# Batch 0's two v loads move ahead of the identity in GpSimd's queue

## The chip, the cores and the metric

The kernel runs on one core of a Trainium2 chip. A core has engines that run side by side, each with its own stream of instructions in order: TensorE (PE, with its weight loads shown as PEld), VectorE (DVE), ScalarE (ACT), GpSimd (POOL) and SyncE (SP). Transfers between main memory and the core's own memory are issued by SP, ACT or GpSimd, each into a queue of its own, and are carried out by the core's 16 DMA engines. The metric is the device time of one execution in microseconds; the time before is the median of three runs, 201.05 us.

## What is computed

Linear attention over 8 batches and 8 heads (sequence 576, head size 64), and behind it a channel-mixing layer (512 to 1024 to 512). Cut to what matters:

```python
q_s = softmax(q, axis=-1)              # over the head's 64 columns
k_s = softmax(k, axis=2)               # over the 576 positions
kv  = einsum('bhsd,bhse->bhde', k_s, v)
x   = einsum('bhsd,bhde->bhse', q_s, kv)   # -> [8, 576, 512]

x_prev = x moved down by one position
xk = mu_k * x + (1 - mu_k) * x_prev
xr = mu_r * x + (1 - mu_r) * x_prev
k  = maximum(xk @ w_k, 0)
out = sigmoid(xr @ w_r) * ((k * k) @ w_v)
```

## The kernel before

The work is cut by batch `b` (0 to 7) and by group `g` (0 or 1, each of four heads in two halves 0 and 1). Every piece of work is an operation with a name: `load01q0` is the load of batch 0, group 1, q, half 0; `load00v` and `load01v` are batch 0's two v loads (a whole group each, into the tiles `vb_a` and `vb_b`, converted to bf16 on the way). `expq`, `rsum`, `rrec` and `scale` make the softmax of q; `expk` the exponentials of k; `KV`, `Z` and `T` are matmuls and transposes on TensorE; `X` makes the mixed attention output; `k`, `r` and `v` with a unit number are the matmuls of the channel-mixing layer.

The order of all operations is written out by hand in one string, `ORDER` (line 42). Each token is an operation, in the form `ENGINE!name:place^held`. The program walks through it and emits each operation on its engine, so the string sets the order within each engine's stream. An engine works its stream in order; between engines, semaphores hold an operation back until what it reads is there. Tokens of different engines that stand beside each other in the string do not wait for one another because of that.

At the start these engines have the following to do, each in this order:

- **SP** issues `load01q0`, `load00q0`, `load01q1`, `load00k0`, `load01k1`.
- **ACT** issues the two loads of the mu rows (`rows`), then `load00q1`, `load00k1`, `load01k0`. Then come a table load and a one-element exponential (`warm`, L228), which reads a tile that VectorE sets to zero, and the exponentials of q and k (L326) as their data arrive.
- **GpSimd** builds the 128 by 128 identity (`ident`, L253: a memset and an affine select, in `masks.py`), then issues `load00v` and `load01v` (L217), `load10q0` (raw_e), and further on four loads of w_k and the loads of batch 1 and of the other weights.
- **VectorE** runs `consts` (L235: four memsets and the cast of `pick`, which reads the identity), `zero` (L230: `warm` and `still`), and `late` (L243), and then the sums and scalings of q.
- **TensorE** runs fillers (L292: matmuls on the tile `still`, whose results nobody reads), the product `wide` (L262, which reads `pick` and the mu rows) after the fifth of them, one more filler that is held until batch 0's first reciprocal is done, and more fillers held by exponentials and sums, up to `KV000`.

The raw input tiles are raw_a and raw_b for batch 0's q, raw_c for group 0's k, and raw_d for group 1's k. Batch 0's transposes of q on TensorE read the identity too (L361). The v loads are read by `KV000`, `KV001` (vb_a) and `KV010`, `KV011` (vb_b), at L391.

Of the kernel before, what the change touches and what calls it, by code (L numbers as in the profile page):

```python
# [8 lines left out]
ACT = mybir.ActivationFunctionType  # L9
# [30 lines left out]
FIRST = ((0, 0), (0, 1), (1, 0), (1, 1))  # L40

ORDER = """
ACT!rows ident load01q0:0 load00q0:1 ACT!load00q1 load01q1 load00v consts ACT!load00k1:2 load00k0
ACT!load01k0:3 load01v zero late fill:3 warm load10q0:4 fill.2:2 fill.3:3 wk11 fill.4:2 fill.5:3
wk00 expq000:0 wide:0 load10q1 load01k1 rsum000:0 wk01 rrec000 expq011:1 scale000:0 wk10 expq010
fill.6^rrec000:3 rsum011:1 fill.7^expq011:2 expq001 fill.8^expq010:3 rsum010 fill.9^rsum011:2
fill.31:2 rsum001 fill.10^expq001:3 expk000:0 fill.11^rsum010:2 rrec010 widecopy scale010:1
# [771 lines left out]
```

## Time and profile before

| what | value |
|---|---|
| median of 3 runs | 201.05 us (200.26, 201.05, 202.83) |
| span of the profiled execution | 199.1 us |
| TensorE busy | 187.2 us |
| DMA, 0 to 20 us | 254 GB/s |
| DMA, 40 to 60 us | 400 GB/s |
| DMA, 100 to 120 us | 70 GB/s |

The span runs from the first instruction to the last one of the profiled execution. The profile gives no other time for that execution; the runs were timed without it, and their median is 1.95 us above its span. The median carries what lies around the span as well.

Where each of batch 0's loads stands in the profile (issue: start of the issuing instruction; landing: as the profile gives it from issue):

| tile | queue | issue, us | to landing, us |
|---|---|---|---|
| raw_a (2 loads) | SP | 0.74 and 1.65 | 6.6 (median) |
| raw_b | SP | 1.19 | 3.3 |
| raw_b | ACT | 1.59 | 6.4 |
| raw_c | ACT | 1.99 | 8.6 |
| raw_c | SP | 2.17 | 8.6 |
| raw_d | ACT | 2.49 | not given |
| raw_d | SP | 3.72 | not given |
| vb_a | GpSimd | 1.44 | 9.4 |
| vb_b | GpSimd | 2.29 | 11.2 |

In lines of the profile, `out<-in` are the tiles written and read; a bracket at the end of a timeline line holds the idle time of the engine just before the instruction, and what ended it. Engine idle time costs something only where the end of the kernel hangs on it.

### The profile page before, as it was taken

Reading aid. Unit: us, or ns where it says so; the run is one execution under the profiler, and the core shown is the slowest. Engines: PE = TensorE matmul, PEld = TensorE weight load, DVE = VectorE, ACT = ScalarE, POOL = GpSimd, SP = SyncE. Lnnn points to the kernel's source line nnn. Section 1 sums busy time; section 2 is a strip of 40 time slices with the busy share of each in tenths; the row PEclk is TensorE's granted clock in tenths of the full one; section 3 lists DMA queues with packets and bytes.
Section 4 is the critical chain, followed back from the end, with each engine's and each line's share of the span. In section 5 each row is a group of like instructions: output and inputs, shape, how many; then the busy total and the mean of one; then the engine's idle time right before and its main releaser. Section 6 shows DMA issues by size and latency. Waiting matters only on the chain.

```text
span 199.1 us, 5164 instructions
## 1 busy us (share of the span) xinstructions
PE 187.2 (94%) x2059; PEld 92.3 (46%) x2085; DVE 150.8 (76%) x348; ACT 145.7 (73%) x224; POOL 43.6 (22%) x70
## 2 busy tenths in 40 slices
PE   6598999989999999999999999999999999999992
PEld 2045445434444444445565545544444544444751
DVE  1588486889989999999999995999825459732531
ACT  3377798799999999999999488777624762552340
POOL 8435438954424312622000000000000000000000
PEclk9999999999999999999999999999999999999999
DMA  6999999999999998799942130422044013402513
GB/s 199 256 276 281 279 336 230 367 397 393 415 393 395 400 407 328 243 412 405 376 116 54 45 90 0 102 63 54 3 105 107 0 23 85 105 2 53 121 40 105
DMA packets 16544, 40.13 MB, mean 202 GB/s; under 512 B 2300, under 2 KB 5640, under 8 KB 16520
## 3 DMA queue, kind: packets, MB, share of 16 engines
q0 software_dynamic: 9440, 27.99, 42.3%
q1 hardware_dynamic: 6400, 10.65, 19.5%
q10 hardware_dynamic: 680, 1.15, 1.6%
q8 instruction: 16, 0.26, 0.6%
q14 instruction: 8, 0.07, 0.1%
HBM read 33.56 MB, written 9.44 MB: 216 GB/s over the span
## 4 chain that ended last, share of the span: by engine, by line
PE 50%; issue 1%; ACT 0%; DVE 0%
PE mm_c L653 7%; PE mm_d L653 6%; PE mm_d L601 5%; PE mm_c L601 4%; PE mm_a L653 4%; PE mm_b L601 4%; PE mm_a L601 4%; PE mm_b L633 3%; PE mm_b L653 3%; PE mm_a L633 3%; PE mm_d L633 2%; PE mm_c L633 1%; PE att_b L517 1%; PE att_a L517 1%; PE att_a L391 1%
## 5 line engine op out<-in xcount | busy, mean ns | idle before, releaser
L653 PEld LDWEIGHTS <-k_a 128*128 128x128 bf16 x144 | 13.8, 98 | 16.9 <-DVE k_a L592 0.6
L633 PEld LDWEIGHTS <-xr 128*128 128x128 bf16 x144 | 13.9, 98 | 16.4 <-issue 0.2
L653 PEld LDWEIGHTS <-k_b 128*128 128x128 bf16 x152 | 14.3, 98 | 15.0 <-issue 0.6
L633 PE MATMUL mm_b<-wr,xr 128*128 128x512 bf16 x45 | 12.2, 379 | 0.2
L601 PEld LDWEIGHTS <-wk_bb 128*128 128x128 bf16 x80 | 7.8, 98 | 7.7
L601 PEld LDWEIGHTS <-wk_ba 128*128 128x128 bf16 x80 | 7.7, 98 | 7.8 <-issue 0.3
L601 PEld LDWEIGHTS <-wk_ab 128*128 128x128 bf16 x80 | 7.6, 98 | 8.0 <-DVE xk L489 0.5
L601 PEld LDWEIGHTS <-wk_aa 128*128 128x128 bf16 x80 | 7.4, 98 | 8.3 <-issue 1.0
L633 PE MATMUL mm_a<-wr,xr 128*128 128x512 bf16 x39 | 10.2, 379 | 0.1
L588 ACT ACTIVATE rel_a<-mm_b 128x512 bf16<-128x512 f32 (+1 forms) x10 | 5.8, 576 | 5.9 <-PE mm_b L601 5.9
L588 ACT ACTIVATE rel_c<-mm_c 128x512 bf16<-128x512 f32 (+1 forms) x11 | 6.6, 598 | 1.2 <-PE mm_c L601 1.2
L633 PE MATMUL mm_c<-wr,xr 128*128 128x512 bf16 x28 | 7.2, 379 | 0.0
L592 DVE TENSOR_TENSOR k_b<-rel_a 128x512 bf16<-128x512 bf16 (+1 forms) x13 | 5.2, 401 | 2.4 <-ACT rel_a L588 2.0
L633 PE MATMUL mm_d<-wr,xr 128*128 128x512 bf16 x27 | 7.0, 379 | 0.0
L592 DVE TENSOR_TENSOR k_a<-rel_c 128x512 bf16<-128x512 bf16 (+1 forms) x14 | 5.7, 404 | 1.6 <-ACT rel_c L588 1.5
L592 DVE TENSOR_TENSOR k_b<-rel_c 128x512 bf16<-128x512 bf16 (+1 forms) x14 | 5.4, 387 | 1.8 <-ACT rel_c L588 1.4
L292 PE MATMUL mm_d<-still 128*128 128x512 bf16 x8 | 4.7, 592 | 2.1 <-DVE still L233 1.9
L592 DVE TENSOR_TENSOR k_a<-rel_b 128x512 bf16<-128x512 bf16 (+1 forms) x12 | 4.9, 404 | 2.4 <-ACT rel_b L588 2.4
L588 ACT ACTIVATE rel_c<-mm_b 128x512 bf16<-128x512 f32 (+1 forms) x6 | 3.5, 578 | 4.3 <-PE mm_b L601 4.3
L292 PE MATMUL mm_c<-still 128*128 128x512 bf16 x8 | 4.5, 611 | 2.2 <-ACT eq_b L326 2.2
L601 PE MATMUL mm_c<-xk,wk_ab 128*128 128x512 bf16 (+1 forms) x22 | 6.1, 361 | 0.3 <-DVE xk L489 0.2
L592 DVE TENSOR_TENSOR k_a<-rel_a 128x512 bf16<-128x512 bf16 (+1 forms) x14 | 5.4, 388 | 1.2 <-ACT rel_a L588 1.1
(358 smaller groups left out, 555.2 us busy)
## 6 DMA issues: line engine op xcount, KB each, us to landing
out_dram<-th_a SPq DMA_DIRECT2D x13, 128.0 KB, 4.6
out_dram<-th_b SPq DMA_DIRECT2D x12, 128.0 KB, 4.0
out_dram<-th_c SPq DMA_DIRECT2D x10, 128.0 KB, 2.8
out_dram<-th_d SPq DMA_DIRECT2D x10, 128.0 KB, 2.4
out_dram<-th_e SPq DMA_DIRECT2D x10, 128.0 KB, 3.9
raw_k<-in_v_dram POOLq DMA_DIRECT2D x2, 576.0 KB, 6.9
raw_a<-in_q_dram POOLq DMA_DIRECT2D x2, 576.0 KB, 10.0
raw_b<-in_q_dram POOLq DMA_DIRECT2D x2, 576.0 KB, 9.9
```

Source lines behind the costliest of these rows:

```text
L292: return kn.nc.tensor.matmul(kn.bank(slot), lhsT=kn.still[:, 0:128], rhs=kn.still[:], start=True, stop=True)
L391: kn.nc.tensor.matmul(kn.half(slot, r)[two[u], KVO:KVO + n], lhsT=kn.eks[ek.index][two[r], j, u, :], rhs=by, start=(j == 0), stop=(j == J ...
L517: kn.nc.tensor.matmul(kn.half(slot, u)[two[r], to:to + n], lhsT=kn.ws[w.index][two[u], r, :], rhs=kn.qts[qt.index][two[u], r, 64 + at:64 + ...
L588: kn.nc.scalar.activation(out=kn.rels[rel.index][:, 0:n], in_=kn.bank(kf)[:, 0:n], func=ACT.Relu, scale=HALF_ROOT)
L592: kn.nc.vector.tensor_tensor(out=kn.k2s[k2.index][:, fc, 0:n], in0=kn.rels[rel.index][:, 0:n], in1=kn.rels[rel.index][:, 0:n], op=ALU.mult)
L601: kn.nc.tensor.matmul(kn.bank(kf)[:, 0:n], lhsT=kn.wk[fc // 4][ct % 2][:, ct // 2, (fc % 4) * 128: (fc % 4) * 128 + 128], rhs=kn.xs[0][:, ...
L633: kn.nc.tensor.matmul(kn.bank(rps), lhsT=kn.xs[1][:, ct, c:c + 128], rhs=kn.wr[:, ct, :], start=(ct == 0), stop=(ct == CT - 1))
L653: kn.nc.tensor.matmul(kn.bank(vps)[:, 0:width], lhsT=kn.k2s[k2.index][:, ft, 128 * m:128 * m + 128], rhs=wv_of(ft)[:, part], start=(ft == ...
```

## The change

In `ORDER`, the token `ident` moves from the second place to behind `load01v`, and `load01v` moves up to stand right behind `load00v`. GpSimd's stream then begins with the two v loads, and the identity follows. All loads of GpSimd keep their order among each other, as do those of SP and ACT; the streams of VectorE and TensorE stay as they are.

```diff
 ORDER = """
-ACT!rows ident load01q0:0 load00q0:1 ACT!load00q1 load01q1 load00v consts ACT!load00k1:2 load00k0
-ACT!load01k0:3 load01v zero late fill:3 warm load10q0:4 fill.2:2 fill.3:3 wk11 fill.4:2 fill.5:3
+ACT!rows load01q0:0 load00q0:1 ACT!load00q1 load01q1 load00v load01v ident consts ACT!load00k1:2
+load00k0 ACT!load01k0:3 zero late fill:3 warm load10q0:4 fill.2:2 fill.3:3 wk11 fill.4:2 fill.5:3
```

## The prediction

> **What bounds the kernel now.** I read the page's engine table and the chain of waits first, then the busy time by stage, the timeline of the first 20 us, who waited for whom, and the DMA queues window by window.
>
> ```profile
> PE 187.2 (94%) x2059; PEld 92.3 (46%) x2085; DVE 150.8 (76%) x348; ACT 145.7 (73%) x224; POOL 43.6 (22%) x70
> ...
> PE 50%; issue 1%; ACT 0%; DVE 0%
> ```
>
> TensorE is busy 94% of the span and the chain that ended last consists of matmuls. By stage:
>
> ```profile
> 0.00:20.00 20.00, 14.78 (x216) 6.71 (x220) 12.09 (x47) 11.40 (x18) 10.46 (x21) 1.00 1.00 254
> 20.00:40.00 20.00, 19.90 (x231) 9.58 (x232) 14.61 (x36) 16.96 (x29) 13.20 (x22) 1.00 1.08 303
> ```
>
> The columns are the stage, its length, the busy time of PE, PEld, DVE, ACT and POOL with counts, the clock, the DMA share and GB/s. From 20 us on PE has no room (19.90 of 20). Only before that does it wait, and the DMA share there is 1.00: the start waits for data, and the end of the kernel moves with the moment at which the dense part begins. So I ask which load that moment hangs on.
>
> ```profile
> 8.31 1.26 ACT L326 ACTIVATE eq_b<-raw_a 128x576 bf16<-128x576 f32 x2 [3.12 <-DMA raw_a<-in_q_dram]
> ...
> 13.19 1.26 ACT L326 ACTIVATE ek_b<-raw_d 128x576 bf16<-128x576 f32 x2 [0.62 <-DMA raw_d<-in_k_dram]
> 14.35 1.10 ACT L369 COPY qt_a<-att_b 128x1152 bf16<-128x1152 bf16 x1
> ```
>
> Each line has start, length, instruction, and in brackets the idle time and what ended it. The last k loads (raw_d) release ScalarE at 13.19; then come its copy at 14.35, the first K·V product of group 1 on PE at 14.69, and everything behind. The two v loads are not in this chain: vb_a was issued at 1.44 and took 9.4 us to land (10.84), its first use is at 12.99; vb_b, issued at 2.29, took 11.2 (13.49), first use 14.69. They have 2.15 and 1.20 us to spare.
>
> **The change, part by part.** GpSimd's queue now:
>
> ```profile
> 0.74 0.20 POOL masks.py:197 MEMSET ident<- 128x128 bf16 x1 [0.29 <-POOLq L803]
> 1.02 0.29 POOL masks.py:199 TENSOR_SCALAR_AFFINE_SELECT ident<-ident 128x128 bf16<-128x128 bf16 x1
> 1.44 0.85 POOL L217 DMA_DIRECT2D vb_a<-in_v_dram  x1
> 2.29 0.74 POOL L217 DMA_DIRECT2D vb_b<-in_v_dram  x1
> 3.01 0.60 POOL L202 DMA_DIRECT2D raw_e<-in_q_dram  x1
> ```
>
> Nothing is added or removed. The issues of vb_a and vb_b move 1.44 - 0.74 = 0.70 us forward, the identity moves back by 0.85 + 0.74 = 1.59: done at 1.31 + 1.59 = 2.90 instead of 1.31. From raw_e on the queue is as it was, since the sum of what stands ahead is the same. SP's and ACT's queues issue nothing later: none of their loads waits for the identity.
>
> *The later identity.* VectorE's next instruction after its first four memsets is the cast of `pick` (1.34), which reads the identity. It goes to 2.93, and behind it in order stand `zero` (the one-element memset `warm` at 1.50, the `still` memset ending at 1.84) and `late` (until 2.04). These move to 3.1 to 3.6 us. Three users:
> - ACT's table load at 2.95 belongs to the warm-up exponential, which reads `warm`. If it waits, it starts near 3.15 and the first exponential near 4.7 instead of 4.51. After that exponential ACT is idle 3.12 us until 8.31, so this costs nothing.
> - VectorE's first row sum goes from 5.23 to about 5.4; its next work begins at 9.03, after 2.00 us of idle time. Nothing.
> - PE's five fillers start at 3.5 instead of 1.90, the mu product L262 (2.07 us at 4.14) at 5.7, filler 6 (6.29, 0.61) at about 7.9. It ends near 8.5, still before 9.05, where the next filler waits 2.15 us for ACT. The cover left is 0.55 us. `widecopy` reads the mu product only at 11.41. The transposes need the identity at 13.58. Nothing.
>
> *The earlier v loads.* Their gain is nothing, since v has 1.20 us to spare and raw_d releases the chain. What they can cost is the q and k loads' share of the DMA engines. The DMA queues window by window (queue, packets, MB, share of 16 engines; q1 is SP's, q10 ACT's, q0 GpSimd's), first 2 to 5 us, then 5 to 6, then 8 to 10:
>
> ```profile
> q1 hardware_dynamic: 331, 0.69, 74.4%
> q10 hardware_dynamic: 142, 0.28, 27.1%
> ```
>
> ```profile
> q0 software_dynamic: 63, 0.07, 53.2%
> q1 hardware_dynamic: 49, 0.09, 26.9%
> q10 hardware_dynamic: 10, 0.02, 8.3%
> ```
>
> ```profile
> q1 hardware_dynamic: 125, 0.26, 38.2%
> q0 software_dynamic: 122, 0.13, 37.7%
> q10 hardware_dynamic: 123, 0.26, 33.9%
> ```
>
> Until 5 us GpSimd's queue has moved no packet, though vb_a was issued at 1.44; SP and ACT move 473 packets in 3 us, 158 per us. Then v joins and takes a third. SP and ACT together move 59 in 5 to 6, 143 in 6 to 8, 248 in 8 to 10, 202 in 10 to 12, and 18 after 12: 670 in all, 93 per us over the seven full ones, 112 per us from 8 to 12. The raw_d loads are the last of these.
>
> If the first v packet comes 0.70 us earlier, with the issue, 0.70 x 158 = 111 packets of SP and ACT that went alone must go beside GpSimd's. At 112 per us they take 0.99 us, 0.29 more than before; at 93 per us (if the slow stretch of 5 to 8 us is lengthened, not only shifted) 1.19, 0.49 more. That v is through earlier gives nothing back, because behind it in the same queue stand raw_e and the weights, which take the same third. Raw_d lands 0.29 to 0.49 us later; I take 0.4, between the two, as nothing tells them apart. No slack on the path takes it up: ACT was already waiting for raw_d. From 18.65 us on PE never waits over 0.4 us for one thing, so it reaches the end nearly whole.
>
> How early v's first packet can be is not shown by the trace. From below: not earlier than now, 0.0. From above: a load issued into an empty queue at 79.20 us (raw_g) shows its first packets between 80.6 and 80.8, 1.4 us after its issue; from 0.74 that is 2.1, which is 2.9 us ahead of 5.0. Then 2.9 x 158 = 458 packets go beside v, at 112 to 93 per us, +1.2 to +2.0 us. I keep to the shift by the issue, because the row nearest to it is this same first load, which took more than 3.5 us. The Trainium skill ("DMA: Bandwidth & Descriptors", Latency and other measured facts) gives about 1 us to the first byte of a GpSimd load; here the trace shows 3.5, and it decides. By the page v would move from 1.74 us, and the same working gives an estimate of +1.3 to +2.3.
>
> **Sum.** 0 + 0.4 on the span of 199.1 gives 199.5. The page gives no time of its own for the profiled execution; the runs' median of 201.05 is 1.95 above the span, and with that 201.45, say 201.4 us.
>
> **Rivals.**
> 1. *The change does not reach the end*: the first v packet stays near 5 us whatever the issue time, because something else holds GpSimd's queue back (the long first load speaks for it). 201.05. Chance 0.18.
> 2. *v gets onto the engines at about 2.1 us*, as an undisturbed load does, and every q and k load gives way from the start: +1.2 to +2.0, 202.3 to 203.1. For it: the first load's long delay falls together with SP's and ACT's loads being ahead of it. Chance 0.14.
> 3. *Faster*: the DMA share is 0.53 and 0.71 in the two half microseconds from 1.5 to 2.5, so there is idle engine time to fill. If v's packets get in there, and less of v is left in the way when raw_d goes through, raw_d lands sooner. It gains at most ACT's idle 0.62 us before raw_d; it decides if raw_d lands before 12.57. 200.45. Against it: no v packet by 5 us. Chance 0.08.
> 4. *The matmul clock.* Fillers start 0.43 us apart up to 12.16, matmuls after 19 us 0.22: PE changed pace in between, by the shorter starts near 12.99, though the page's clock row reads 9 throughout. If q lands later, the fillers from 9.05 on start later and the step may come late: the work from 12.99 to 16.2, 2.6 us busy, would take up to twice as long. Up to 203.7. Chance 0.05.
> 5. *The identity is much later than 2.90*, because GpSimd finishes it only after the loads' descriptors are out. After the identity come the cast, `warm`, table load, warm exponential and first exponential, about 2.5 us; ACT is free until 8.31, so that matters from 5.8 us on, by as much as it is later. The one slow thing on GpSimd here is the first load's 3.6 us from issue (1.44) to after 5.0; if both loads hold the identity for that long, it is done at 0.74 + 7.2 + 0.5 = 8.4, and the end is 2.6 later, 204.0. Against it: vb_b's issue followed vb_a's after 0.85 us, and the identity took 0.29. Chance 0.04. The Trainium skill ("GPSIMD Engine Reference", Instruction dispatch) names a first-call load of code of about 6 us without a visible instruction; by that page an estimate of 2.3 + 6 = 8.3 us for the identity comes out. No such gap stands before the identity in this trace: its reader ran at 1.34.
>
> **How the numbers follow.** The forecast has the remaining 0.51, and 201.4. The range goes from 200.2 (rival 3, and the runs' own scatter of 200.26 to 202.83) to 203.2 (the top of rival 2). Two per cent of 201.05 is 4.0 us, about what a measurement of this kernel can tell from no change. No single case reaches it; slower needs rivals 2 and 4 together or an identity near 10 us: 0.06. Nothing in the profile is worth 4 us of gain; 0.03 for what I have not seen. Within 2%: 0.91.
>
> **What would show it.** The two v issues at 0.74 and about 1.6, the identity done near 2.9, PE's first filler near 3.5, all with no wait behind them: the moves are free. GpSimd's first packets in 4 to 5 us and ACT's exponentials of raw_d starting at 13.5 to 13.7: the forecast. First packets at 2 to 3 us: rival 2. Raw_d before 13.19: rival 3. It would be wrong altogether if the dense part began where it does now and the end still moved.

## The result and the profile after

The changed kernel takes 202.73 us (median of 19 runs, 200.71 to 204.25), the kernel before 201.14 us (19 runs beside it, 199.27 to 202.83). The ratio is 1.0083 with a 95% interval of 1.0060 to 1.0105: slower by 0.8%, clear of zero and well inside the 2% that count here as no change. The ratio is taken from the executions in the faster of two states alone, so it is not quite the quotient of the two medians. The profiled execution after took 202.36 us, with a span of 200.6, which is 1.5 us more than the span of 199.1 before.

First the page's engine table and chain, and the busy time by stage, of the changed kernel (columns as before: stage, length, busy time of PE, PEld, DVE, ACT and POOL, clock, DMA share, GB/s):

```profile
PE 187.8 (94%) x2059; PEld 92.7 (46%) x2085; DVE 151.0 (75%) x348; ACT 145.8 (73%) x224; POOL 43.4 (22%) x70
...
PE 50%; issue 1%; ACT 0%; DVE 0%
```

```profile
0.00:20.00 20.00, 13.79 (x206) 6.39 (x212) 11.03 (x42) 10.72 (x17) 10.46 (x21) 1.00 1.00 256
20.00:40.00 20.00, 19.84 (x226) 9.50 (x224) 14.21 (x38) 17.24 (x30) 11.57 (x19) 1.00 1.06 299
```

TensorE's work has not grown by anything that matters (187.8 us against 187.2). In the first 20 us it is busy for 13.79 us instead of 14.78, from then on it is as dense as before. The loss arises at the start. GpSimd's timeline there, now:

```profile
1.25 0.85 POOL L217 DMA_DIRECT2D vb_a<-in_v_dram  x1 [0.81 <-POOLq L803]
2.10 0.75 POOL L217 DMA_DIRECT2D vb_b<-in_v_dram  x1
2.82 0.24 POOL masks.py:197 MEMSET ident<- 128x128 bf16 x1
3.14 0.29 POOL masks.py:199 TENSOR_SCALAR_AFFINE_SELECT ident<-ident 128x128 bf16<-128x128 bf16 x1
3.38 0.58 POOL L202 DMA_DIRECT2D raw_e<-in_q_dram  x1
```

The first v load does not move into the identity's place at 0.74. GpSimd sits idle for 0.81 us and issues it at 1.25, only 0.19 us earlier than before (1.44). Before, the identity was built inside that gap. ScalarE's timeline shows what came of it:

```profile
4.58 0.68 ACT L326 ACTIVATE eq_a<-raw_b 128x576 bf16<-128x576 f32 x1
9.46 1.26 ACT L326 ACTIVATE eq_b<-raw_a 128x576 bf16<-128x576 f32 x2 [4.20 <-DMA raw_a<-in_q_dram]
...
13.64 1.26 ACT L326 ACTIVATE ek_b<-raw_d 128x576 bf16<-128x576 f32 x2
15.70 1.12 ACT L369 COPY qt_a<-att_b 128x1152 bf16<-128x1152 bf16 x1 [0.80 <-PE att_b L361]
```

The first exponential behind the pause is 1.15 us later (9.46 against 8.31). It reads the second half of raw_a, SP's third load, which now lands 7.8 us after its issue instead of 6.6. The raw_d exponentials start at 13.64, only 0.12 us after the end of the one before them, and the copy behind them now waits 0.80 us for TensorE. So raw_d does not hold the start of the dense part here; TensorE's own order does. Its timeline, first before, then after (fillers are L292, the products with v are L391):

```profile
9.05 0.61 PE L292 MATMUL mm_c<-still 128*128 128x512 bf16 x1 [2.15 <-ACT eq_b L326]
...
12.16 0.90 PE L292 MATMUL mm_c<-still 128*128 128x512 bf16 x2
12.99 0.66 PE L391 MATMUL att_a<-vb_a,ek_a 64*64 64x64 bf16 x36
13.58 0.44 PE L361 MATMUL att_b<-ident,qs_a 64*128 64x64 bf16 x18
...
14.69 0.21 PE L391 MATMUL mm_a<-vb_b,ek_b 64*64 64x64 bf16 x1
```

```profile
10.20 0.61 PE L292 MATMUL mm_c<-still 128*128 128x512 bf16 x1 [1.32 <-ACT eq_b L326]
...
13.30 1.06 PE L292 MATMUL mm_c<-still 128*128 128x512 bf16 x2
14.29 0.99 PE L391 MATMUL att_a<-vb_a,ek_a 64*64 64x64 bf16 x36
15.21 0.44 PE L361 MATMUL att_b<-ident,qs_a 64*128 64x64 bf16 x18
...
16.33 0.21 PE L391 MATMUL mm_a<-vb_b,ek_b 64*64 64x64 bf16 x1
```

From the late exponential hangs a chain of nine fillers, 0.43 us apart, and behind them in TensorE's order the first product with v. The fillers begin 1.15 us later; the product begins 1.30 later and takes 0.99 us instead of 0.66; the transposes begin 1.63 later. The last line of each is group 1's product, which needs raw_d's exponentials. It stands 1.11 us behind the transposes before (13.58 to 14.69) and 1.12 after (15.21 to 16.33), although in the second case those exponentials had ended 1.4 us earlier (14.90). So raw_d did not hold TensorE before either, and the path into the dense part ran through the second half of raw_a and the fillers in both kernels.

The offset stays: the first matmul with `wk_aa` goes from 18.65 to 20.29, and a matmul that waits for `mu` further on from 42.98 to 44.62, 1.64 us each. Of this, 1.15 are the late q data, 0.15 the last of the nine fillers (now at the slow spacing) and 0.33 the slower product.

Why q is late can be seen in the DMA queues from 4 to 5 us (queue, packets, MB, share; q0 is GpSimd's, q1 SP's, q10 ACT's). First before, then after:

```profile
q1 hardware_dynamic: 64, 0.14, 64.9%
q10 hardware_dynamic: 92, 0.18, 46.9%
```

```profile
q10 hardware_dynamic: 108, 0.21, 61.8%
q0 software_dynamic: 36, 0.04, 28.8%
q1 hardware_dynamic: 19, 0.03, 9.0%
```

Before, GpSimd's queue had no packet in this microsecond; now it has 36, and SP's queue drops from 64 to 19 while its q loads are under way. The first v packets appear between 4.4 and 4.6 us now, between 5.0 and 5.2 before.

### The profile page after: what moved, and what is told of

Its sections match the earlier page's. It is cut to its first block, busy times and chain, and to the rows that moved or that the text cites. A ratio compares the mean times of both kernels' runs of the same rounds, so it can differ in the third digit from the quotient of the medians.

```text
span 200.6 us, 5164 instructions
## 1 busy us (share of the span) xinstructions
PE 187.8 (94%) x2059; PEld 92.7 (46%) x2085; DVE 151.0 (75%) x348; ACT 145.8 (73%) x224; POOL 43.4 (22%) x70
## 3 DMA queue, kind: packets, MB, share of 16 engines
q10 hardware_dynamic: 680, 1.15, 1.7%
## 4 chain that ended last, share of the span: by engine, by line
PE 50%; issue 1%; ACT 0%; DVE 0%
PE mm_c L653 7%; PE mm_d L653 6%; PE mm_d L601 5%; PE mm_c L601 4%; PE mm_a L653 4%; PE mm_b L601 4%; PE mm_a L601 4%; PE mm_b L633 3%; PE mm_b L653 3%; PE mm_a L633 3%; PE mm_d L633 2%; PE mm_c L633 1%; PE att_b L517 1%; PE att_a L517 1%; PE att_a L391 1%
## 5 line engine op out<-in xcount | busy, mean ns | idle before, releaser
L653 PEld LDWEIGHTS <-k_a 128*128 128x128 bf16 x144 | 13.7, 98 | 17.0 <-DVE k_a L592 0.6
L292 PE MATMUL mm_d<-still 128*128 128x512 bf16 x8 | 4.7, 591 | 4.2 <-DVE still L233 4.0
L292 PEld LDWEIGHTS <-still 128*128 128x128 bf16 x18 | 2.0, 123 | 10.3 <-DVE still L233 4.0
```

The costliest lines, as they stand in the source:

```text
L292: return kn.nc.tensor.matmul(kn.bank(slot), lhsT=kn.still[:, 0:128], rhs=kn.still[:], start=True, stop=True)
L653: kn.nc.tensor.matmul(kn.bank(vps)[:, 0:width], lhsT=kn.k2s[k2.index][:, ft, 128 * m:128 * m + 128], rhs=wv_of(ft)[:, part], start=(ft == ...
```

## The experiments

Two theories. **A**: v's earlier packets push back the q and k loads of SP and ACT, and the chain above carries that to the end. **B**: the identity, finished at 3.43 instead of 1.31, holds up the fillers (first one at 4.02 instead of 1.90) and with them TensorE's pace. All ratios are to the kernel before, run beside each experiment on the same chip in five rounds. The experiments fall into four groups, each on another chip, and the changed kernel itself was not run again beside them, so a ratio set against its 1.0083 is a comparison between measurements. A spare identity is an identity in a tile that nobody reads; fillers are read by nobody either, so no run changes what is computed.

### Each part of the change alone

*v first, but the fillers not held up*, on the changed kernel:

```diff
-... load00v load01v ident consts ... ACT!load01k0:3 zero late
+... load00v load01v zero ident consts ... ACT!load01k0:3 late
```

> The changed kernel, with VectorE's two memsets for the fillers and for the warm-up (`zero`) ahead of the ones that wait for the identity. The v loads stay first in GpSimd's queue. Theory A (v's earlier packets push back the q and k loads): as the changed kernel, ratio to before 1.006 to 1.010, ACT's exponential of raw_a's second half near 9.4 us. Theory B (the late identity holds up the fillers, and with them TensorE's pace): back to before, ratio 0.998 to 1.002.

Measured: 1.0065 (1.0040 to 1.0090). The first filler ran at 1.23 us, and the loss stayed. (The profile of this kernel is of the slowest of its 12 runs, 204.0 us against a median of 202.51.)

*The identity late, but v not earlier*, on the kernel before:

```diff
-ACT!rows ident load01q0:0 ... load00v consts ... load01v zero
+ACT!rows spare load01q0:0 ... load00v load01v ident consts ... zero
```

> Only the identity is late: a spare identity is built first on GpSimd, then the v loads are issued as early as before (1.44 us), then the identity that is used is built (done near 3.5 us). GpSimd's further loads come 0.55 us later. Theory A: ratio 0.998 to 1.002, exponential of raw_a's second half near 8.3 us. Theory B: ratio 1.006 to 1.010, first product of group 0 with v near 14.3 us.

Measured: 1.0011 (0.9989 to 1.0034). ScalarE's first exponential behind the pause, in the first of these runs and in the second:

```profile
10.96 1.25 ACT L326 ACTIVATE eq_b<-raw_a 128x576 bf16<-128x576 f32 x2 [5.56 <-DMA raw_a<-in_q_dram]
```

```profile
8.27 1.26 ACT L328 ACTIVATE eq_b<-raw_a 128x576 bf16<-128x576 f32 x2 [3.16 <-DMA raw_a<-in_q_dram]
```

With v early it is late, with v at 1.44 us it is where it was (8.31), although the identity was then as late as in the changed kernel (first filler at 4.20). A holds, B falls: the late identity by itself costs at most 0.34%, the top of the interval. The run also puts GpSimd's further loads off by 0.55 us, more than the change does (raw_e's issue went from 3.01 to 3.38), so those are not the cause either. One line of this speaks against a clean story: the product with v took 0.99 us in the second run too, where nothing was lost. The slow pace at that place comes without the loss as well.

### v at other times

One, two and four spare identities between the identity and the v loads:

```diff
-ACT!rows ident load01q0:0
+ACT!rows ident spare spare.2 load01q0:0
```

> One spare identity between the identity and the v loads: issued near 2.0 us, between the kernel before (1.44) and the run with two spares (2.5). Theory A with a smooth price: exponential of raw_a's second half near 8.0 us, ratio 0.998 to 1.001. With a threshold between 1.25 and 1.44 us: 7.6 to 8.3 us, ratio as with two spares, 0.997 to 1.001.

> The other way round: identity as before, then two spare identities, then the v loads, which are issued near 2.5 us, one us later than before. Theory A: the q and k loads get the engines for longer, exponential of raw_a's second half near 7.5 us, ratio 0.993 to 0.999 as long as v still lands before it is used (vb_b had 1.2 us to spare). Theory B: no effect from v, ratio 0.998 to 1.002.

> Four spare identities ahead of the v loads, issued near 3.6 us. Theory A: the exponential of raw_a's second half comes near 7.5 us, but vb_a lands near 13.2 us, after it is wanted, so the gain is spent: ratio 0.999 to 1.004. If v's place does not matter at all: 0.998 to 1.001 with the exponential near 8.3 us.

Only the first of the two v loads ahead of the identity, on the changed kernel:

```diff
-... load00v load01v ident consts
+... load00v ident load01v consts
```

> Only vb_a's load ahead of the identity, vb_b's behind it (issued near 2.7 us; in the changed kernel 2.10, in the kernel before 2.29). Theory A, with the first packets deciding: SP's third load still lands late (over 7.3 us after its issue at 1.65), ratio 1.003 to 1.009. If the whole of v has to be early: near 6.6 us after its issue, ratio 0.998 to 1.002.

Another load of GpSimd's queue (288 KB, no conversion) ahead of the identity, and v behind it:

```diff
-ACT!rows ident load01q0:0 ... warm load10q0:4
+ACT!rows load10q0:4 ident load01q0:0 ... warm
```

> Another load first: the kernel before with batch 1's first q load (raw_e, no conversion of type) ahead of the identity on GpSimd, and the v loads behind the identity, issued near 2.6 us. Theory A in its wide form (whatever GpSimd's queue sends first displaces SP's q loads): exponential of raw_a's second half near 9.4 us or later, ratio 1.004 to 1.010. Narrow form (only the v loads with their conversion do that): near 8 us, ratio 0.997 to 1.002.

All of them, with the packets of GpSimd's and SP's queues from 4 to 5 us in one profile each, and the start of the first exponential behind the pause in the same profile:

| kernel | v issued, us | GpSimd, SP packets in 4 to 5 us | exponential at, us | ratio (interval) |
|---|---|---|---|---|
| changed kernel | 1.25, 2.10 | 36, 19 | 9.46 | 1.0083 (1.0060 to 1.0105) |
| one v load first | 1.25, 2.63 | 36, 28 | 9.06 | 1.0062 (1.0039 to 1.0085) |
| before | 1.44, 2.29 | 0, 64 | 8.31 | 1 |
| one spare | 1.76, 2.60 | 0, 82 | 9.16 | 1.0006 (0.9985 to 1.0027) |
| two spares | 2.51, 3.35 | 0, 64 | 7.66 | 0.9987 (0.9965 to 1.0010) |
| four spares | 3.75, 4.59 | 0, 91 | 6.92 | 0.9984 (0.9965 to 1.0004) |
| other load first (1.27) | 2.50, 3.23 | 48, 26 | 8.31 | 1.0020 (0.9991 to 1.0050) |

The price falls to nothing between an issue at 1.25 and one at 1.44 us: it is there when the first v load goes out at 1.25 and v's packets come before 5 us, whole, as far as the intervals tell, when only vb_a's do, and it is not seen with v at 1.44 or later. No issue between the two was tried, nor one before 1.25, so whether this is a step or a steep slope is not shown. Later than before, v brings nothing that can be told from zero. With four spares the q and k data do come earlier (first exponential at 6.92 us, vb_a lands 7.9 us after its issue, at 11.65), and the first `wk_aa` matmul begins at 17.99 instead of 18.65; but the span is 199.2. The gain lasts until a wait that the kernel before does not have:

```profile
41.92 0.73 PE L481 MATMUL att_b<-qt_a,wp_b 64*64 64x288 bf16 x8 [0.60 <-POOL wp_b L469]
```

In the kernel before, the same matmul starts at 41.92 too, so the whole gain is gone there. GpSimd computes `wp_b` at 41.40 in this run and at 40.28 before, behind the issue of a load that also comes later (40.66 against 39.53). That this goes back to its loads starting 2.3 us later is likely and not shown.

The other load ahead of v came to 1.0020, between the two forms of A, and its interval holds both "no price" and 0.5%. It puts v off by one us as well, so wide and narrow form stay untold apart. In its profile SP's queue falls to 26 packets too and the exponential still comes at 8.31, while GpSimd's queue moves only 9 packets from 5 to 6 us, against 70 in the changed kernel. So the count in 4 to 5 us alone does not decide when q lands.

Each profile shows one execution, and these scatter. Over all fourteen profiles the first exponential behind the pause starts at 8.45 to 10.96 us in the six with v first (issued at 1.24 to 1.25), at 8.27 to 8.69 in the three with v at 1.44, and at 6.92 to 9.16 in the five with v later. Where it is late, that same execution is long: the span is 199.1 us with the exponential at 8.31, 200.2 at 9.16 (one spare, an execution of 202.02 us against a median of 201.33), 200.6 at 9.46 and 202.2 at 10.96 (the run with `zero` first). Below 8.3 nothing more is gained: 199.0 at 7.66, 199.2 at 6.92. That ties the end of the kernel to this exponential, whatever makes it late. The price of the change is read from the ratios.

### Fillers and pace

Three of the nine fillers taken out of the changed kernel:

```diff
-fill.31:2 rsum001 ... expk001 fill.13:2 fill.32:2 rrec011
+rsum001 ... expk001 rrec011
```

> The changed kernel without three of the nine fillers between the q exponentials and the first product with v (fill.31, fill.13, fill.32; their results are read by nobody). If the chain of fillers is what holds that product back (0.43 us each at the slow pace), it starts up to 1.3 us earlier, near 13.2 us, and the ratio to before falls to 1.000 to 1.005. If not, the ratio stays at 1.006 to 1.010; if fewer fillers delay TensorE's faster pace, it rises above that.

Measured: 1.0057 (1.0034 to 1.0080), inconclusive in time, since its interval overlaps the changed kernel's. Its profile tells more: from the first of the remaining fillers to the product with v it is 2.89 us (11.43 to 14.32) instead of 4.09, so the chain did hold the product back, but raw_c's exponential, which ended at 13.73, then stood next. (This execution took 203.09 us, against a median of 202.28.)

Five fillers more, right behind the sixth, so that TensorE works through its pause, in the kernel before and in the changed one:

```diff
-fill.6^rrec000:3
+fill.6^rrec000:3 fill.18:2 fill.19:3 fill.20:2 fill.21:3 fill.22:2
```

> The kernel before, with five more fillers behind the sixth, so that TensorE works through its 2.15 us pause ahead of 9.05 us. If the slow pace of TensorE costs time between 9 and 16 us, it changes to the faster pace before the nine fillers are through, these take 0.22 instead of 0.43 us each, the first product with v starts near 12.2 us (behind raw_c's exponentials) and the ratio to before is 0.993 to 0.997. If the pace there costs nothing, 0.999 to 1.001.

> The same five fillers in the changed kernel. If part of its loss is the slow pace (fillers, and the products of group 0 with v, 0.99 us instead of 0.66), the ratio to before falls from 1.0083 to 1.001 to 1.004. If the loss is the late q data alone, it stays at 1.006 to 1.010.

Measured: before 0.9993 (0.9963 to 1.0023), an interval that reaches into both ranges of its expectation and settles neither; changed kernel 1.0040 (1.0020 to 1.0060), of which these are TensorE's lines:

```profile
12.95 0.61 PE L292 MATMUL mm_d<-still 128*128 128x512 bf16 x1
13.38 0.40 PE L292 MATMUL mm_c<-still 128*128 128x512 bf16 x1
13.62 0.38 PE L292 MATMUL mm_d<-still 128*128 128x512 bf16 x1
13.83 0.59 PE L292 MATMUL mm_c<-still 128*128 128x512 bf16 x2
14.36 0.66 PE L391 MATMUL att_a<-vb_a,ek_a 64*64 64x64 bf16 x36
```

The spacing falls from 0.43 to 0.22 us between two fillers, and the product is back at 0.66 us. About half of the loss is gone at the centre of the intervals, 1.0083 to 1.0040; the intervals just touch, so the size of that share is not settled. The profile shows less than half: the first `wk_aa` matmul begins at 20.02 instead of 20.29, and the span is 200.3 instead of 200.6. The Trainium skill ("TensorE: Matmul & The Clock Gate", Part 1) has TensorE's clock halve after an idle window of some 3.4 us and double after a busy one, and these windows run on by themselves, not from the kernel's start. The halved and full spacing (0.43 and 0.22 us) agree with that here. The faster pace does not come at a fixed time behind the pause: some 3.9 us in the kernel before (9.05 to 12.99) and some 5 us in the changed one (10.20 to 15.21). No run here shows the length of the window, and the clock row of the profile's page, at 9 throughout, does not show the change of pace.

The same with v at 2.51 us, three fillers more:

```diff
-ACT!rows ident load01q0:0 ... fill.6^rrec000:3
+ACT!rows ident spare spare.2 load01q0:0 ... fill.6^rrec000:3 fill.18:2 fill.19:3 fill.20:2
```

> The v loads issued near 2.5 us behind two spare identities, and three more fillers behind the sixth, so that TensorE works through its pause ahead of 8.4 us. If late q data and the slow pace are both in the time, the first product with v starts when vb_a has landed (near 12.2 us) and the next one at vb_b's landing (near 13.7 us, not 14.7), and the ratio to before is 0.992 to 0.997. If v's landing then holds everything, 0.997 to 1.001.

Measured: 1.0009 (0.9986 to 1.0032). Neither gain appeared. In its profile the added fillers ran when the nine should have (the sixth filler started only at 7.81, held by a q load that landed late), and the product with v began at 13.34. No version was found that is faster than the kernel before by more than its interval.

### Which load is it

Two q loads exchanged in the changed kernel, so that what the first exponential waits for comes from ACT's queue:

```diff
-load00q0:1 ACT!load00q1 load01q1 load00v
+load00q0:1 ACT!load01q1 load00q1 load00v
```

> The changed kernel with two q loads exchanged: ACT's first q load is now raw_a's second half (which the first exponential behind the pause waits for), SP's third is raw_b's second half (which the third one waits for). Theory A, in the form that SP's third load is the one displaced: the first exponential behind the pause starts near 6 to 8 us, raw_b's second half lands over 7 us after its issue, only five of the nine fillers are still behind it, and the ratio falls to 1.001 to 1.005. If all loads are late alike: 1.006 to 1.010.

Measured: 1.0094 (1.0058 to 1.0130). No gain, as expected if all loads are late alike. The profile is of the fastest of its six runs (201.45 us, median 202.87), so it shows little of the loss. In it the first exponential came at 8.45, SP's third load was again the slow one (now of raw_b, 8.0 us after its issue), but a filler further on had to wait for k:

```profile
12.67 0.61 PE L292 MATMUL mm_d<-still 128*128 128x512 bf16 x1 [0.60 <-ACT ek_a L326]
```

So the loss does not hang on SP's third load alone. That raw_c, which is late too (its first exponential at 11.93, before 10.82), takes over where raw_a's second half is out of the way is a reading of this one profile and not shown for the slower runs.

## Why the prediction was right, and where it was wrong

The range (200.2 to 203.2 around 201.4) and the side held: v's packets in front of q and k cost, the rest is free. The path and with it the size were wrong: 0.4 us was forecast and 1.59 measured, four times as much. That 202.73 lies in the range is owed to the upper end, which came from rival 2 and not from the forecast's own sum. Step by step:

- **The later identity costs nothing**: right, shown by the run with only that part (1.0011). Its times were off: done at 3.43 us, not 2.90, first filler at 4.02, not 3.5, because the queue ahead of it began 0.51 us later than I put it. The table load (2.96) did not wait for `warm`.
- **v's issue moves 0.70 us forward**: wrong. It moved 0.19. I took the first place in the queue for the time at which the identity's memset starts; the trace of before could not show that a load cannot start there. What the idle 0.81 us are spent on stays open: the profile names only the queue's own instructions.
- **Packets in 4 to 5 us**: right (36), in part by luck. The issue moved by 0.19 us, but the first v packet by 0.4 to 0.8 in these two profiles (seen first between 5.0 and 5.2 before, between 4.4 and 4.6 after), near the 0.70 of the sum. Why it moved more than the issue stays open.
- **Raw_d releases the chain**: wrong, and the step that failed. Raw_d itself did what I said: its exponentials start at 13.64, in the forecast of 13.5 to 13.7. But TensorE did not wait for them, even before. The wait of 0.42 us that the profile puts down to raw_d's exponential (the weight load for group 1's product, at 14.68) stands in the same length after the change, where that exponential was long done, and the product follows the transposes at 1.11 and 1.12 us. The way into the dense part was SP's third q load, its exponential and nine fillers in order, up to the first product with v. I had read the fillers as cover that costs nothing.
- **+0.4 us**: mis-sized by that. The span grew by 1.5 us, the median by 1.59. SP's third q load came 1.15 us later, not 0.3 to 0.5; the last filler and the slower product added 0.15 and 0.33. Mean packet rates, which I used, do not give the landing of one load: they gave raw_d's (0.45 later) and missed this one by more than half a microsecond.
- **The sum's 1.95 us** between span and time: every run listed since has both, and they lie 1.72 to 1.85 apart. The profiled execution before was thus a little faster than the median; the change of 1.5 to 1.6 us does not hang on it.
- **Rival 1** (no effect) falls with the interval. **Rival 2** named the right size (+1.2 to +2.0) but not the mechanism: no v packet came before 4 us in the profile of the changed kernel. **Rival 3** (faster) falls. **Rival 4**, the pace, was at work beside the forecast, by 0.4% from the centre of one interval to that of the other (1.0083 and 1.0040), by 0.3 us between the two profiles. **Rival 5** falls: 3.43 us.

A rule stands beside the main finding: by the Trainium skill ("DMA: Bandwidth & Descriptors", Queues, rings and completion order) each DMA engine takes packets from its queues in turn, so a queue that joins takes a share from the others. The counts from 8 to 10 us before (125, 122, 123) agree. Those from 4 to 5 us after (108, 36 and 19) are not even, and no run here shows why SP's queue lost most. The rule does not give the landing time of a load; that had to be measured.

## What to carry to other kernels

An early load in an idle queue is not free when the engines behind all queues are full: ask which loads are needed first, and let the ones with time to spare come behind them. Before pricing a delay by one load, check that the engine at the end really waits for it: a wait that a profile puts down to a load can be there without it. Follow the engine's own order back, fillers included, to the load that its first work hangs on. The start of a queue is not the start of its first load: look in the trace for what really holds the first issue before moving it.

## What was not expected of the hardware

- GpSimd's first load started at 1.24 to 1.27 us in all seven kernels that had a load at the head of that queue, after 0.80 to 0.82 us of idle time, while a memset at the head started at 0.74. An identity of 0.57 us (0.74 to 1.31) ahead of it puts the load off by 0.19 us only.
- GpSimd's first v packet is on the engines some 3 us after the load's issue: issued at 1.25 it is first seen between 4.4 and 4.6 us in the changed kernel, issued at 1.44 between 5.0 and 5.2 in the kernel before. This scatters too: with five fillers more in the changed kernel one packet is there between 3.5 and 3.8. The other load, without conversion, was issued at 1.27 and first seen between 3.4 and 3.6. The 1.4 us of the load issued at 79.20 us are less sure than the prediction has them: the queue was not empty, since 17 of its packets still went from 79.2 to 80.
- A shift of 0.19 us in the issue was worth 0.8% of the time, while 2.3 us in the other direction (1.44 to 3.75) was worth nothing that could be measured.
